# Attention beside a gated linear unit on one core: in the last unit, the values' products as two sets of 64 rows in two PSUM banks

## The chip, the core and the metric

The kernel runs on one core of one Trainium2 chip. Its time is the device time in microseconds (us) of one execution; several executions give a median. The profile is that of one execution, with its records laid out by engine: PE is TensorE (PEld its weight loads), DVE is VectorE, ACT is ScalarE, POOL is GpSimd and SP is SyncE, which issues the DMAs.

## What is computed

The reference mixes two branches over the same `x` (2048 rows of 512) by a gate for each row. Branch A is attention with 32 query heads of width 16 that share one key head and one value head, followed by an output projection. Branch B is a linear unit with a sigmoid gate and an inner width of 1792. All is float32.

```python
q = (x @ wq).reshape(B, S, 32, 16).transpose(0, 2, 1, 3)
k, v = x @ wk, x @ wv
p = softmax(einsum("bhqd,bkd->bhqk", q, k) * 16 ** -0.5)
a = einsum("bhqk,bkd->bhqd", p, v).transpose(0, 2, 1, 3).reshape(B, S, 512) @ wo
b = (sigmoid(x @ w_gate) * (x @ w_up)) @ w_down
g = sigmoid((x * gate_w).sum(-1, keepdims=True))
return g * a + (1 - g) * b
```

## The kernel before

**Units and chunks.** The queries are worked in 32 units (NU): four blocks of 512 rows, and eight groups of four heads in each. A unit walks over 16 chunks (NC) of 128 keys. Of each chunk there are four score matmuls, one for each head (`scores`, L1096 to L1103, the matmul at L1101), with the keys in the rows and one 64-row half of TensorE's array each; two in opposite halves make a pair. ScalarE takes the exponential of each from its PSUM bank into an SBUF tile `p` of 128 keys by 512 queries (L1103). Row maxima are found ahead of it by another pass of matmuls whose banks VectorE reduces (`maximum`, L1087 to L1094); the last unit's maxima are done before the stretch that this study looks at.

**The values' products.** `pv` (L974 to L977) takes the four `p` tiles of one chunk. Each is the moving operand of one f32 matmul over all 128 rows; the stationary operand is the chunk of `v_aug`, 128 keys by 32 columns (16 values and ones that sum the exponentials). Head j writes partitions 32j to 32j + 31 of one bank, so four column tiles share the array. Such a matmul leaves two records in the profile: 32 units by 16 chunks by 4 heads are 2048 matmuls, and L977 has 4096 records. A unit's chunks are worked in runs, one to six chunks at a time, between scores and the matmuls of branch B and of the output projection (`fill`, L1060 to L1071, in opposite halves too). In the units before the last, each run's sums leave the bank by a ScalarE copy (L984) and are added up on GpSimd (L991). The last unit, number 31, keeps one bank open from its first chunk to its last.

**What orders the work.** The order on every engine is written out by hand: the string `ORDER` (L645 to L690) has a letter or hex digit for each step, `V` for the values of one chunk, hex digits for pairs of half-row matmuls. `plan` (L693) plays it on a `State`, which keeps planned times, hands out the eight PSUM banks (`take`, L173 to L178: the one that comes free first) and places the work of the other engines (`settle`, L395). Each engine then runs its instructions in that order and waits on semaphores for what it needs; at the end of the program the order is pinned (L1153 to L1161). A score's matmul waits until the exponential of the score that had its bank before is done. In the stretch at hand the banks hold scores, the open sums of the values, and the open sums of the output projection of the last block of rows (`wa`), one for each half.

**The last unit and the end.** The last unit's 16 chunks are worked in ten runs: chunk 0 directly behind the last chunks of unit 30; 1; 2; 3; 4 and 5; 6; 7 and 8; 9 and 10; 11 and 12; 13 to 15. Until the run of 7 and 8 begins, the projection's `wa` matmuls are worked between the scores, and ScalarE takes a scaled copy of their sums now and then (L1052). Then only scores and values are left. Behind the last chunk come twelve half-row matmuls of the last projection (`we`, L1071), each three of which VectorE adds to the output (L1034). The end of the kernel (L1122 to L1150) then serves the last unit: ScalarE copies the sums' bank in two halves of 256 columns (L1128), four transposes bring queries into the rows (L1130), VectorE takes reciprocals (L1135) and divides (L1137), two more transposes (L1139), copies (L1141), four f32 matmuls with the last rows of `wo` in opposite halves (L1144), and VectorE's last sums (L1148) with their stores.

Of the kernel before, what the change touches and what calls it, by code (L numbers as in the profile page):

```python
# [12 lines left out]
ALU = mybir.AluOpType  # L13
# [5 lines left out]
P = 128  # L19
# [5 lines left out]
NC = S // P  # L25
NG = H // 4
NU = NB * NG
# [8 lines left out]
HALF = (TOP, BOT)  # L36
# [75 lines left out]
class State:  # L112
# [60 lines left out]
    def take(self):  # L173

        i = self.free.index(min(self.free))
        assert self.free[i] <= self.now
        self.free[i] = NEVER
        return i  # L178
# [325 lines left out]
    def issue_v(self):  # L504
        u, c = divmod(self.vp, NC)
        if self.sum is None:
            self.sum = self.take()
        self.run_of.append(["values", u, c, not self.run_of, False, self.sum])
        self.acts.append(self.run_of[-1])
        self.now += VALUES  # L510
        self.done += VALUES
        self.held -= 4
        self.exps.pop(0)
        self.vp += 1
        if c == NC - 1:
            self.release()
# [176 lines left out]
def plan():  # L693
    s = State()
    for code in ORDER:
        s.step(code)
    return s.acts
# [3 lines left out]
def tile_kernel(ctx, tc, x_in, wq, wkv, wo, wg, wu, wd, consts_in, out):  # L701
    nc = tc.nc
# [13 lines left out]
    banks = [pp.tile([P, 512], F32, tag=f"bank{i}", name=f"bank{i}") for i in range(8)]  # L716
# [136 lines left out]
    v_aug = cp.tile([P, NC, 32], F32, name="v_aug")  # L853
# [117 lines left out]

    PT, VD, OT = {}, {}, {}

    def pv(u, c, start, stop, ps):  # L974

        for j in range(4):
            nc.tensor.matmul(ps[32 * j:32 * j + 32, :], v_aug[:, c, :], PT.pop((u, c, j)), start=start, stop=stop)  # L977

    SUMS, PARTS_OF = {}, {}
# [116 lines left out]
    def scores(h, n, i):  # L1096
# [8 lines left out]
    on_bank = lambda act: lambda *args: act(*args[:-1], banks[args[-1]])  # L1105
# [4 lines left out]
        "load": load_item, "w_hi": w_hi, "w": w_split, "x_hi": x_hi, "x": x_lo, "turn_x": turn_x,  # L1110
        "f": fill, "gate": gate, "gated": gated, "h": h_split, "part": part_of, "add": add_part, "out": send_out,
        "m": maximum, "max_finish": max_finish, "max_turn": on_bank(max_turn), "send_max": send_max, "s": scores,
        "values": on_bank(pv), "finish": on_bank(finish), "store": store, "sums": sums, "invert": invert, "send_inverse": send_inverse,
        "spread": spread, "divide": divide,
    }
    for what, *args in plan():
        acts[what](*args)
        if what == "values":
            end = args[-1]


    n0 = (NB - 1) * NT  # L1122
    spare = lambda name: ap.tile([P, TB], F32, tag="p", name=name, bufs=PB)
    end, rest = banks[end], [bank for i, bank in enumerate(banks) if i != end]
    ps = rest[3:]
    ou = [spare(f"ou_last{i}")[:, :2 * P] for i in range(2)]
    for i in range(2):
        nc.scalar.copy(ou[i], end[:, i * 2 * P:(i + 1) * 2 * P])  # L1128
    for t in range(NT):
        nc.tensor.transpose(rest[t // 2][:, part(t % 2)], ou[t // 2][:, part(t % 2)], ident)  # L1130
    o = []
# [68 lines left out]
```

## Time and profile before

| | |
|---|---|
| Times of three runs | 1600.48, 1600.30, 1599.23 us; median 1600.3 us |
| The profiled execution's own time | 1598.83 us |
| Its span, first to last instruction | 1597.1 us |
| Granted TensorE clock | 1.0 of full speed |
| Matmuls of the values, L977 | 4096 records, 491.3 us busy, mean 598 ns |
| Score matmuls, L1101 | 2048, mean 400 ns |
| Exponentials, L1103 | 2048, mean 652 ns |
| DMA | 102.31 MB, 64 GB/s over the span |

A timeline row has the start in us from the span's start, the length in us, engine, line, operation, the tiles (output <- inputs), shapes, and how many instructions follow each other under that row (x); in brackets the engine's idle time before it and what ended it. Lengths of records overlap: a matmul's record reaches to its last output, and the next one starts earlier, so the distance between starts is the time that the engine needs for one. The same is true of ScalarE and VectorE, whose records begin while the instruction ahead is still at work. A row of busy times has, for each engine, the us in which it was busy in the stretch and the number of instructions in it.

### The profile page before, as it was taken

To read this page: it belongs to the slowest core of one execution; us is meant where nothing else is said; L and a number is where in the kernel's file an instruction comes from. 1 tells how busy PE (TensorE), PEld (TensorE's weight loads), DVE (VectorE), ACT (ScalarE), POOL (GpSimd) and SP (SyncE) were. 2 spreads that over 40 slices of the span, in tenths; PEclk is the share of its full clock that TensorE was granted. 3 is DMA by queue.
4 is the path that set the end of the run, shared out by engine and by line. 5 is a ranking of instruction groups with operands and counts; after the bars stand their busy time and mean duration, and the time that the engine had idled before them with its cause. 6 is when DMAs were issued, how large, how long until landed. Compare 5 with 4: busy or idle time off the path is not lost.

```text
span 1597.1 us, 33902 instructions
## 1 busy us (share of the span) xinstructions
PE 1587.9 (99%) x12918; PEld 998.6 (63%) x12918; DVE 1392.0 (87%) x2372; ACT 1258.4 (79%) x2474; POOL 848.0 (53%) x708
## 2 busy tenths in 40 slices
PE   9999999999999999999999999999999999999998
PEld 7776665665656566566666566666656665656654
DVE  7999998998988989988998898889989998988832
ACT  4268778888878878879878877878987887878896
POOL 4254364558363664375745446454936366536463
PEclk9999999999999999999999999999999999999999
DMA  7621121115111212013411121111502021201111
GB/s 239 216 80 42 42 57 36 45 59 137 29 68 32 75 56 60 18 39 83 111 37 58 39 75 54 55 38 59 137 28 68 32 75 46 71 16 42 34 36 44
DMA packets 54678, 102.31 MB, mean 64 GB/s; under 512 B 18232, under 2 KB 19768, under 8 KB 53492
## 3 DMA queue, kind: packets, MB, share of 16 engines
q1 hardware_dynamic: 54516, 100.16, 21.0%
q8 instruction: 101, 1.65, 0.4%
q14 instruction: 61, 0.50, 0.1%
HBM read 74.05 MB, written 13.09 MB: 55 GB/s over the span
## 4 chain that ended last, share of the span: by engine, by line
PE 98%; ACT 0%; DVE 0%; DMA 0%; POOL 0%; issue 0%; DVEq 0%
PE bank L1071 31%; PE bank L977 29%; PE bank L1092 18%; PE bank L1101 16%; PE bank L838 4%; ACT p L1103 0%; PE bank L963 0%; PE bank L908 0%; DVE ba L1148 0%; DVE ba L1034 0%; DMA wkv_raw<-wkv 0%; POOL wkv_s L732 0%; DVE wkv_stack L869 0%; PE bank L1144 0%; DVEq L1196 0%
## 5 line engine op out<-in xcount | busy, mean ns | idle before, releaser
L1094 DVE TENSOR_REDUCE mx<-bank 128x1 f32<-128x512 f32 x2048 | 1257.4, 681 | 133.8 <-PE bank L1092 80.5
L1103 ACT ACTIVATE p<-bank 128x512 f32<-128x512 f32 x2048 | 1050.1, 652 | 2.6 <-PE bank L1101 0.4
L1101 PE MATMUL bank<-qs,ks 64*128 64x512 f32 x2048 | 698.0, 400 | 0.0
L1092 PE MATMUL bank<-ks,qs 62*128 62x512 f32 x2048 | 686.6, 406 | 0.0
L977 PE MATMUL bank<-p,v_aug 128*32 128x512 f32 x4096 | 491.3, 598 | 0.7 <-ACT p L1103 0.7
L1092 PEld LDWEIGHTS bank<-ks,qs 62*128 62x128 f32 x2048 | 338.4, 184 | 151.3 <-issue 51.1
L1101 PEld LDWEIGHTS bank<-qs,ks 64*128 64x128 f32 x2048 | 345.7, 185 | 105.5 <-ACT p L1103 29.9
L991 POOL TENSOR_TENSOR ou<-ou,ou 128x512 f32<-128x512 f32 x201 | 259.0, 1289 | 204.9 <-ACT ou L984 199.2
L984 ACT COPY ou<-bank 128x512 f32<-128x512 f32 x232 | 140.9, 608 | 266.6 <-PE bank L977 122.2
L1071 PE MATMUL bank<-wd,hl 64*128 64x512 f32 x1344 | 273.5, 393 | 0.0
L977 PEld LDWEIGHTS bank<-p,v_aug 128*32 128x32 f32 x4096 | 107.7, 109 | 232.2 <-issue 188.1
L1071 PEld LDWEIGHTS bank<-wd,hl 64*128 64x128 f32 x1344 | 195.0, 185 | 20.4 <-ACT p L1103 1.7
L1071 PE MATMUL bank<-xs,wg 64*128 64x512 f32 x672 | 203.2, 393 | 0.0
L1071 PE MATMUL bank<-xs,wu 64*128 64x512 f32 x672 | 199.7, 393 | 0.0
L1071 PE MATMUL bank<-x,wu 64*128 64x512 f32 x672 | 194.5, 391 | 0.0
L1071 PE MATMUL bank<-x,wg 64*128 64x512 f32 x672 | 190.4, 391 | 0.0
L1071 PEld LDWEIGHTS bank<-xs,wg 64*128 64x128 f32 x672 | 119.7, 185 | 8.1
L1071 PEld LDWEIGHTS bank<-xs,wu 64*128 64x128 f32 x672 | 118.6, 185 | 7.3
L1071 PEld LDWEIGHTS bank<-x,wu 64*128 64x128 f32 x672 | 115.5, 185 | 10.7 <-issue 1.7
L1071 PEld LDWEIGHTS bank<-x,wg 64*128 64x128 f32 x672 | 113.3, 185 | 9.4 <-POOL wu L814 0.8
L1055 POOL TENSOR_TENSOR ba<-ba,pa_d 128x512 f32<-128x512 f32 x48 | 61.8, 1288 | 95.9 <-DVE ba L1034 62.6
L813 POOL CAST wu<-ru 128x1024 fp32r<-128x1024 f32 x27 | 28.1, 1039 | 117.6 <-PE bank L1071 94.3
(83 smaller groups left out, 1064.1 us busy)
## 6 DMA issues: line engine op xcount, KB each, us to landing
rg<-wg SPq DMA_DIRECT2D x28, 512.0 KB
ru<-wu SPq DMA_DIRECT2D x28, 512.0 KB
rd<-wd SPq DMA_DIRECT2D x28, 512.0 KB
qs<-qd SPq DMA_DIRECT2D x192, 64.0 KB
qd<-q SPq DMA_DIRECT2D x32, 256.0 KB
xs<-x SPq DMA_DIRECT2D x16, 512.0 KB
xf<-x_in SPq DMA_DIRECT2D x16, 256.0 KB
ra<-wo SPq DMA_DIRECT2D x8, 512.0 KB
```

Source lines behind the costliest of these rows:

```text
L813: nc.gpsimd.tensor_copy(WS[item][:, 0, :], raw)
L838: nc.tensor.matmul(ps, w[:, p, part(kc)], X[b, kc][:, q, :], start=i == 0, stop=i == 3 * KC - 1)
L977: nc.tensor.matmul(ps[32 * j:32 * j + 32, :], v_aug[:, c, :], PT.pop((u, c, j)), start=start, stop=stop)
L984: nc.scalar.copy(to, ps)
L991: nc.gpsimd.tensor_tensor(SUMS[u], SUMS[u], PARTS_OF[u].pop(0), op=ALU.add)
L1055: nc.gpsimd.tensor_tensor(BA[b, t], BA[b, t], PA.pop((b, t)), op=ALU.add)
L1071: nc.tensor.matmul(banks[i], l, r, start=at == 0, stop=at == j.n - 1)
L1092: nc.tensor.matmul(banks[i], qs_t[u % 3][r, pr, part(qt)], ks[r, kb * 512:(kb + 1) * 512], start=True, stop=True)
L1094: nc.vector.tensor_reduce(MX[u][:, pr, h, qt, kb:kb + 1], banks[i], axis=AX.X, op=ALU.max)
L1101: nc.tensor.matmul(banks[i], ks[r, part(c)], qs_t[u % 3][r, pr, :], start=True, stop=True)
L1103: nc.scalar.activation(p, banks[i], AF.Exp, scale=0.25)
```

## The change

In unit 31 alone, each chunk's product is worked as two sets of four matmuls: the first over key rows 0 to 63 into one bank, the second over rows 64 to 127 into a second bank. Both banks stay open over all 16 chunks, so the planner takes one bank more at the unit's first chunk; where no bank is free at the planned time, its clock moves on to the time at which one is. At the end ScalarE copies the first bank as before, and VectorE adds the second bank to each half of the copy before the transposes. Banks are numbered otherwise from then on, and the order of the instructions on each engine is otherwise that of before: TensorE has 64 matmuls more, VectorE the two adds.

```diff
     def take(self):
         i = self.free.index(min(self.free))
+        if self.vp >= (NU - 1) * NC:
+            self.now = max(self.now, self.free[i])
         assert self.free[i] <= self.now
...
         if self.sum is None:
             self.sum = self.take()
+            if u == NU - 1:
+                self.other = self.take()
...
+        if u == NU - 1:
+            self.run_of[-1][0] = "halves"
+            self.run_of[-1].append(self.other)
...
-    def pv(u, c, start, stop, ps):
-
-        for j in range(4):
+    def pv(u, c, start, stop, ps, *other):
+
+        for h, bank in enumerate((ps, *other) if other else ()):
+            for j in range(4):
+                nc.tensor.matmul(bank[32 * j:32 * j + 32, :], v_aug[HALF[h], c, :], PT[u, c, j][HALF[h]],
+                                 start=start, stop=stop)
+        for j in range(0 if other else 4):
             nc.tensor.matmul(ps[32 * j:32 * j + 32, :], v_aug[:, c, :], PT.pop((u, c, j)), start=start, stop=stop)
...
-    end, rest = banks[end], [bank for i, bank in enumerate(banks) if i != end]
-    ps = rest[3:]
+    two, rest = [banks[i] for i in end], [bank for i, bank in enumerate(banks) if i not in end]
+    ps = [rest[3], two[0], rest[4], rest[5]]
...
     for i in range(2):
-        nc.scalar.copy(ou[i], end[:, i * 2 * P:(i + 1) * 2 * P])
+        nc.scalar.copy(ou[i], two[0][:, i * 2 * P:(i + 1) * 2 * P])
+        nc.vector.tensor_tensor(ou[i], ou[i], two[1][:, i * 2 * P:(i + 1) * 2 * P], op=ALU.add)
```

More of the change, by code (lines that the diff above doesn't have):

```diff
@@ L1112, in tile_kernel @@
         "m": maximum, "max_finish": max_finish, "max_turn": on_bank(max_turn), "send_max": send_max, "s": scores,
-        "values": on_bank(pv), "finish": on_bank(finish), "store": store, "sums": sums, "invert": invert, "send_inverse": send_inverse,
+        "values": on_bank(pv), "halves": lambda u, c, a, b, *two: pv(u, c, a, b, *(banks[i] for i in two)), "finish": on_bank(finish), "store": store, "sums": sums, "invert": invert, "send_inverse": send_inverse,
         "spread": spread, "divide": divide,
@@ L1117, in tile_kernel @@
         acts[what](*args)
-        if what == "values":
-            end = args[-1]
+        if what == "halves":
+            end = args[-2:]
     n0 = (NB - 1) * NT
     spare = lambda name: ap.tile([P, TB], F32, tag="p", name=name, bufs=PB)
-    end, rest = banks[end], [bank for i, bank in enumerate(banks) if i != end]
-    ps = rest[3:]
+    two, rest = [banks[i] for i in end], [bank for i, bank in enumerate(banks) if i not in end]
+    ps = [rest[3], two[0], rest[4], rest[5]]
     ou = [spare(f"ou_last{i}")[:, :2 * P] for i in range(2)]
     for i in range(2):
-        nc.scalar.copy(ou[i], end[:, i * 2 * P:(i + 1) * 2 * P])
+        nc.scalar.copy(ou[i], two[0][:, i * 2 * P:(i + 1) * 2 * P])
+        nc.vector.tensor_tensor(ou[i], ou[i], two[1][:, i * 2 * P:(i + 1) * 2 * P], op=ALU.add)
     for t in range(NT):
```

## The prediction

> **What bounds the kernel now.** The page first, for its span, the busy times and the chain that ended last.
>
> ```profile
> span 1597.1 us, 33902 instructions
> PE 1587.9 (99%) x12918; PEld 998.6 (63%) x12918; DVE 1392.0 (87%) x2372; ACT 1258.4 (79%) x2474; POOL 848.0 (53%) x708
> PE 98%; ACT 0%; DVE 0%; DMA 0%; POOL 0%; issue 0%; DVEq 0%
> ```
>
> Over the whole span TensorE is the bound. But the change touches only the last unit, whose values' products begin at about 1552 us, so I read that stretch by itself: busy times of the window between its first free exponential and its last one, then the chain inside it.
>
> ```profile
> core 0: us, PE busy (x) PEld busy (x) DVE busy (x) ACT busy (x) POOL busy (x), PEclk, DMA share, GB/s
> 1553.43:1583.75 30.32, 29.67 (x239) 13.78 (x235) 3.17 (x5) 30.32 (x61) 15.65 (x15) 1.00 0.11 23
> ```
>
> ```profile
> 1575.80 7.95 ACT p L1103 x16
> ...
> 1583.80 1.06 PE bank L977 x8
> ```
>
> ScalarE is busy 30.32 of 30.32 us there (57 exponentials and four scaled copies): in this stretch it is the bound, and TensorE, though its row says 98%, runs just ahead of it. So an edit on TensorE matters here only if it leaves ScalarE without scores. Behind 1583.75 comes a serial end: the last values, the last output projection, sums, divide, store.
>
> **The rows for the terms.** TensorE's timeline, start and length in us; each matmul of the values leaves two records (two passes), so x8 is one key chunk and x16 two.
>
> ```profile
> 1550.18 2.78 PE L977 MATMUL bank<-p,v_aug 128*32 128x512 f32 x24
> 1552.89 0.49 PE L1101 MATMUL bank<-qs,ks 64*128 64x512 f32 x1
> ...
> 1568.39 0.40 PE L1071 MATMUL bank<-wa,o 64*128 64x512 f32 x2
> 1568.72 1.06 PE L977 MATMUL bank<-p,v_aug 128*32 128x512 f32 x8
> 1569.72 0.72 PE L1101 MATMUL bank<-qs,ks 64*128 64x512 f32 x3
> 1570.06 1.31 PE L1071 MATMUL bank<-wa,o 64*128 64x512 f32 x9
> ...
> 1572.59 0.41 PE L1101 MATMUL bank<-qs,ks 64*128 64x512 f32 x2
> 1572.93 1.92 PE L977 MATMUL bank<-p,v_aug 128*32 128x512 f32 x16
> 1574.78 0.97 PE L1101 MATMUL bank<-qs,ks 64*128 64x512 f32 x6
> ...
> 1583.80 1.06 PE L977 MATMUL bank<-p,v_aug 128*32 128x512 f32 x8 [0.70 <-ACT p L1103]
> 1584.79 3.03 PE L1071 MATMUL bank<-we,o 64*128 64x512 f32 x12
> 1587.75 0.66 PE L1130 MATMUL bank<-consts,ou_last 128*128 128x128 f32 x4
> ...
> 1589.94 1.99 PE L1144 MATMUL bank<-re,o_last 64*128 64x512 f32 x8
> ```
>
> Two chunks last 1574.78 - 1572.93 = 1.85 us, one 1569.72 - 1568.72 = 1.00: a chunk costs **0.86 us**, a run of them 0.14 beside. Pairs of half-row matmuls follow each other 0.23 apart (twelve single ones in 3.03 give 0.25), but the last pair before a run starts 0.33 ahead of it, and the first after it takes 0.34: each run pays about 0.1 + 0.14 + 0.1 = **0.35 us** for going to 32-column tiles and back. ScalarE's timeline:
>
> ```profile
> 1552.23 1.11 ACT L984 COPY ou<-bank 128x512 f32<-128x512 f32 x1
> 1553.42 7.46 ACT L1103 ACTIVATE p<-bank 128x512 f32<-128x512 f32 x15
> 1560.59 0.86 ACT L1052 ACTIVATE pa_a<-bank,gsig 128x512 f32<-128x512 f32 x1
> 1561.16 4.21 ACT L1103 ACTIVATE p<-bank 128x512 f32<-128x512 f32 x8
> 1565.00 0.95 ACT L1052 ACTIVATE pa_a<-bank,gsig 128x512 f32<-128x512 f32 x1
> ...
> 1573.53 0.90 ACT L1052 ACTIVATE pa_a<-bank,gsig 128x512 f32<-128x512 f32 x1
> ```
>
> An exponential takes 0.49 us of ScalarE (8 in 1565.00 - 1561.16 give 0.48, 16 in 7.95 give 0.50), a scaled copy 0.57 (1561.16 - 1560.59).
>
> **The change, part by part.** Each engine keeps its order of instructions: TensorE has 4 matmuls more in each of 16 chunks, VectorE two adds more, and the banks are numbered anew. No DMA, nothing on GpSimd or SyncE moves.
>
> *1. The products.* The 64x32 tile is in no row of before. Each half still streams 512 columns in two passes, so a set of four can't take less than the 0.86 us of today: no gain by itself. If the upper and the lower set run beside each other, a chunk stays at 0.86; if one follows the other, it is 1.72. Two rows speak for beside: the four f32 matmuls at L1144 lie in opposite halves by turns and need 1.99 us, where four in a row would need 4 x 0.86 = 3.44; and four column tiles share one chunk's 0.86 at L977. I take **0**, and keep +0.86 per chunk as the other end.
>
> *2. The switches.* Values and scores are now both of 64 rows, which might spare the 0.35 us per run; or the narrower columns cost it as before. No row shows a change of columns alone. Between 0 and 0.35 I take 0.35, what every run in the rows pays. The Trainium skill (TensorEngine Tiling, Key Properties) says that a change of the tiling mode, not of the tile, drains TensorE, and lists 64x32 and 64x128 as two modes: by that rule the switch stays, which agrees with the 0.35 of the rows and speaks against a gain here. New is one switch between the last chunk of unit 30, still 128 rows, and chunk 0 of unit 31, today one run (x24): about 0.1, with the longer first pass and the eight starts 0.15. ScalarE is out of scores just then (copy until 1553.34, next exponential at 1553.42), so it counts: **+0.15**.
>
> *3. One bank less for scores.* Of eight banks one holds the values' sums and two the output projection's sums in flight until 1572.6; five are left for scores, after the change four. Over a run of two chunks no score is written for 1574.78 - 1572.59 = 2.19 us; a score's exponential starts 0.53 after it (1552.89 to 1553.42), and a bank is TensorE's again about 0.16 after ScalarE has gone on (an exponential's row is 0.60 long at its shortest against 0.49 between them, and 0.05 from 1583.75 to 1583.80). ScalarE must have 2.19 + 0.53 + 0.16 = 2.88 us of work in the banks. Five exponentials and a scaled copy are 5 x 0.49 + 0.57 = 3.02: enough, as the full window shows. Four are 2.53: 0.35 idle. That happens at the runs 1563.41 and 1572.93 (scaled copies at 1565.00 and 1573.53): **+0.7**, between 0 and one exponential each, 1.0. Runs of one chunk need 0.86 less, 2.02 against 4 x 0.49 = 1.96: 0.06 each for four of them, **+0.2**. From 1574 on no projection is in flight, six banks are left, 2.94 against 2.88: nothing. A ScalarE that is full elsewhere can't win any of it back.
>
> *4. The two adds.* VectorE's rows of the end, and the groups by shape:
>
> ```profile
> 1585.86 2.82 DVE L1034 SCALAR_TENSOR_TENSOR ba<-bank,gsig,ba 128x512 f32<-128x512 f32 x4 [12.22 <-PE bank L1071]
> 1588.60 0.20 DVE L1135 RECIPROCAL rc_last<-bank 128x8 f32<-128x8 f32 x1
> ```
>
> ```profile
> L1148 DVE SCALAR_TENSOR_TENSOR ba<-bank,gsig,ba 128x256 f32<-128x256 f32 x2 | 0.9, 480 | 1.5 <-PE bank L1144 1.5
> ...
> L1137 DVE TENSOR_TENSOR on<-bank,rc_last 128x128 f32<-128x128 f32 x2 | 0.6, 290 | 0.1
> ```
>
> The plan's four sums of the last projection are issued ahead of the adds, so these stand in VectorE's queue behind the sum that waits for the twelfth projection matmul. Today the transposes (1587.75, 0.66 long) lie beside that last sum, and the reciprocal starts 0.67 after it has begun (four starts 0.69 apart put it at 1587.93). Afterwards: sum 0.67, first add 0.48 (the 128x256 row; the 128x128 one, 0.29, bounds it below, a 128x512 sum, 0.75, above), 0.05, two transposes 0.44, 0.07: the reciprocal starts 1.71 after it, **+1.05**. The second add (0.40 further) and its transposes lie beside the first half's division. With the adds at 0.29 it is +0.85, at 0.75 +1.3. The two ScalarE copies are done by 1585.6 and hidden. Nothing hides the adds: each step behind them waits for the one before.
>
> Sum: 0.15 + 0.7 + 0.2 + 1.05 = **+2.1 us**. The profiled execution took 1598.8 (span 1597.1 and 1.7 around it), after it 1600.9. The median of the runs shown is 1600.3, 1.5 higher than that execution; against it I forecast **1602.4 us**, 0.13% more. A measurement of this kernel can tell about 0.2%, 3.2 us, from no change.
>
> **The rivals.**
>
> *No switch is paid.* If only the rows count, a run of two needs 2.88 - 0.35 = 2.53 and four banks just do; terms 2 and 3 go to nothing, and the projection behind the last chunk starts 0.2 to 0.3 earlier. The adds stay: +0.8, **1601.1**. For it: all neighbours are of 64 rows. Against it: every run in the rows pays, and none shows which dimension it pays for.
>
> *The sets run one after the other* (the other side: slower). Place: each chunk; price: 0.86; it decides as soon as the tiles of the lower half can't stream while the four of the upper do. 16 x 0.86 = 13.7, less the 0.70 that TensorE waits at 1583.80, with adds, first switch and some starving +14.6: **1614.9**. Then the change doesn't do what it says. Against it the L1144 and L977 rows, but each shows one dimension split, never both.
>
> *The lower set runs one pass late.* If matmuls start strictly in order and both passes of one go ahead of the next, the lower four start 0.43 behind, and each run ends 0.43 later. The two runs of term 3 then lose 0.78 each, the next two 0.37 each, three single ones 0.49, the first 0.58, the last chunk 0.43: 4.8 with the adds' 1.05 **+5.8, 1606.1**. The Trainium skill (TensorE: Matmul & The Clock Gate, Part 3, The mechanism) says that matmuls start and end strictly in the order of the program. The 0.86 of a chunk today, though, has no room for one tile a pass behind another.
>
> *Faster.* The adds alone cost 0.85 to 1.3 and ScalarE has no idle time to give back; to win 3.2 us the exponentials themselves would have to shorten.
>
> **How the numbers follow.** Forecast 0.48; no switch 0.24; one pass late 0.12; one after the other 0.13; faster 0.03. Within 0.2%: 0.48 + 0.24 = 0.72; slower 0.25; faster 0.03. The range runs from 1600.0 (no switch, less the 1.1 by which the runs shown scatter) to 1606.5 (one pass late) and leaves out 0.16.
>
> **What would show it.** A run of two chunks still about 1.9 us with twice the records means term 1 is right; 2.3 the late pass, 3.6 one after the other. The first score pair behind a run still taking 0.34 means the switch stayed; 0.23 that it went. ScalarE idle about 0.35 near 1566 and 1576, and none behind it, shows term 3; a full row refutes it. Two adds between the last sum and the first reciprocal, with 1.7 instead of 0.67 between their starts, show term 4. I am wrong if the time lies in chunks that grew, or in VectorE rows far from 0.48.

## The result, and the profile after

| | before | after |
|---|---|---|
| Median of 18 runs each | 1600.72 us (1599.09 to 1602.18) | 1603.24 us (1601.75 to 1605.31) |
| Ratio of the runs, 95% interval | | 1.0017, 1.001 to 1.0025 |
| The profiled execution's own time, span | 1598.83, 1597.1 us | 1603.01, 1601.2 us |
| Mean granted TensorE clock of the profiled execution | 1.0 | 0.998 |

The changed kernel is **2.5 us slower** (interval 1.6 to 4.0); 1602.4 was forecast. In this kernel `pv`'s 64-row matmul is L985 (L988 over 128 rows), scores are L1112, their exponentials L1114, the projections L1082, scaled copies L1063, the last projection's sums L1045, the adds L1140, the transposes L1142, reciprocal and division L1147 and L1149, the last f32 matmuls L1156.

TensorE's timeline of the changed kernel, columns as before (start, length, engine, line, tiles, shapes, count, idle time before):

```profile
1572.82 0.62 PE L1082 MATMUL bank<-wa,o 64*128 64x512 f32 x4
...
1575.03 1.95 PE L985 MATMUL bank<-p,v_aug 64*32 64x512 f32 x32
1576.90 0.97 PE L1112 MATMUL bank<-qs,ks 64*128 64x512 f32 x6
1577.80 1.95 PE L985 MATMUL bank<-p,v_aug 64*32 64x512 f32 x32
1579.68 1.35 PE L1112 MATMUL bank<-qs,ks 64*128 64x512 f32 x6
1580.96 1.95 PE L985 MATMUL bank<-p,v_aug 64*32 64x512 f32 x32
...
1585.99 1.09 PE L985 MATMUL bank<-p,v_aug 64*32 64x512 f32 x16 [0.30 <-ACT p L1114]
1587.01 3.01 PE L1082 MATMUL bank<-we,o 64*128 64x512 f32 x12
1591.26 0.78 PE L1142 MATMUL bank<-consts,ou_last 128*128 128x128 f32 x4 [1.24 <-DVE ou_last L1140]
1592.32 0.92 PE L1151 MATMUL bank<-consts,on 128*128 128x128 f32 x2 [0.29 <-DVE on L1149]
1593.17 3.35 PE L1156 MATMUL bank<-re,o_last 64*128 64x512 f32 x8
```

A run of two chunks has 32 records instead of 16 and lasts 1.95 us instead of 1.92: the two sets do run beside each other. Two rows are new in kind: the transposes wait 1.24 us for the add, and the last f32 matmuls (x8), 1.99 before, last 3.35. ScalarE's timeline:

```profile
1552.84 1.11 ACT L995 COPY ou<-bank 128x512 f32<-128x512 f32 x1
1554.21 7.81 ACT L1114 ACTIVATE p<-bank 128x512 f32<-128x512 f32 x15 [0.26 <-PE bank L1082]
1561.93 0.69 ACT L1063 ACTIVATE pa_a<-bank,gsig 128x512 f32<-128x512 f32 x1
1562.52 4.04 ACT L1114 ACTIVATE p<-bank 128x512 f32<-128x512 f32 x8
1566.40 0.73 ACT L1063 ACTIVATE pa_a<-bank,gsig 128x512 f32<-128x512 f32 x1
1567.49 4.51 ACT L1114 ACTIVATE p<-bank 128x512 f32<-128x512 f32 x9 [0.37 <-PE bank L1112]
...
1575.23 0.86 ACT L1063 ACTIVATE pa_a<-bank,gsig 128x512 f32<-128x512 f32 x1
1575.80 1.27 ACT L1114 ACTIVATE p<-bank 128x512 f32<-128x512 f32 x2
1577.43 8.50 ACT L1114 ACTIVATE p<-bank 128x512 f32<-128x512 f32 x17 [0.36 <-PE bank L1112]
```

ScalarE, full before, now stands idle twice for 0.36 to 0.37 us, behind the runs of two chunks that were named, and needs 1561.93 - 1554.21 = 7.72 us for the first 15 exponentials (7.17 before, 1553.42 to 1560.59). VectorE's rows of the end:

```profile
1588.07 2.80 DVE L1045 SCALAR_TENSOR_TENSOR ba<-bank,gsig,ba 128x512 f32<-128x512 f32 x4 [12.37 <-PE bank L1082]
1590.79 0.74 DVE L1140 TENSOR_TENSOR ou_last<-ou_last,bank 128x256 f32<-128x256 f32 x2
1591.74 0.21 DVE L1147 RECIPROCAL rc_last<-bank 128x8 f32<-128x8 f32 x1 [0.20 <-PE bank L1142]
...
1595.28 2.85 DVE L1160 SCALAR_TENSOR_TENSOR ba<-bank,gsig,ba 128x256 f32<-128x256 f32 x5 [2.57 <-PE bank L1156]
```

The adds stand where they were expected, and the reciprocal starts 1591.74 - 1590.12 = 1.62 us behind the start of the last sum (1590.12 in the chain of waits of this kernel), 0.67 before. The sums behind the last matmuls wait 2.57 us. Why the last matmuls are slow is told by busy times in two stretches of 3.41 us (each engine's busy time and count, then the granted clock, PEclk):

```profile
1589.12:1592.53 3.41, 1.88 (x9) 0.94 (x8) 3.14 (x9) 0.00 (x0) 0.00 (x0) 1.00 0.00 0
1592.53:1595.94 3.41, 3.30 (x10) 1.37 (x9) 0.84 (x3) 0.53 (x2) 0.00 (x0) 0.50 0.02 5
```

The granted clock was 0.5 from 1592.53 to 1595.94, which holds the last matmuls but for their end. In the profile of before it fell only at 1595.66, when they had long been done; two stretches of that profile ahead of the fall:

```profile
1588.84:1592.25 3.41, 2.57 (x10) 0.96 (x10) 1.84 (x6) 0.53 (x2) 0.00 (x0) 1.00 0.00 0
1592.25:1595.66 3.41, 0.00 (x0) 0.00 (x0) 1.70 (x3) 0.00 (x0) 0.00 (x0) 1.00 0.85 308
```

Nothing of this was forecast.

**Where the time came from, in the trace.** Executions differ ahead of the last unit too: the last run of unit 30 (before: the row at 1550.18) starts between 1550.18 and 1552.85 in the profiles below, a difference that is there within the first 100 us and then stays (one of the kernels below is 2.4 late at 100 us and 2.5 here). In the two profiles that are over 2 us late, TensorE is slow in the first 12 us: nine f32 matmuls that last 2.33 us in before (at 7.33) last 3.46 there in one (the adds early, at 7.80) and 3.74 in the other (TensorE kept busy). So I measure each profile from that start, call it R, to the end of VectorE's last sum:

| us | before | after |
|---|---|---|
| R to the end of the last exponential | 33.56 | 35.13 (+1.57) |
| from there to the start of the last of the four sums | 4.19 | 4.19 |
| from there to the first reciprocal | 0.67 | 1.62 (+0.95) |
| from there to the last f32 matmuls | 1.34 | 1.43 (+0.09) |
| from there to the first final sum | 1.16 | 2.11 (+0.95) |
| from there to the end of VectorE | 2.85 | 2.85 |
| sum | 43.77 | 47.33 (+3.56) |

### The profile page after: what moved, and what is told of

Read it like the earlier page. It is cut to its first block, busy times and chain, and to the rows that moved or that the text cites. A ratio compares the mean times of both kernels' runs of the same rounds, so it can differ in the third digit from the quotient of the medians.

```text
span 1601.2 us, 34160 instructions
## 1 busy us (share of the span) xinstructions
PE 1592.3 (99%) x13046; PEld 1001.2 (63%) x13046; DVE 1392.3 (87%) x2374; ACT 1259.0 (79%) x2474; POOL 848.3 (53%) x708
## 4 chain that ended last, share of the span: by engine, by line
PE 98%; ACT 1%; DVE 1%; DMA 0%; SPq 0%; issue 0%; POOL 0%; DVEq 0%
PE bank L1082 31%; PE bank L988 29%; PE bank L1103 18%; PE bank L1112 15%; PE bank L845 3%; PE bank L985 1%; ACT p L1114 1%; PE bank L970 0%; SPq L958 0%; DMA qs<-qd 0%; DVE ba L1160 0%; ACT x L763 0%; PE bank L1156 0%; DVE ba L1045 0%; DMA wkv_raw<-wkv 0%
## 5 line engine op out<-in xcount | busy, mean ns | idle before, releaser
L1114 ACT ACTIVATE p<-bank 128x512 f32<-128x512 f32 x2048 | 1050.2, 651 | 3.7 <-PE bank L1112 0.9
L1112 PE MATMUL bank<-qs,ks 64*128 64x512 f32 x2048 | 700.2, 401 | 0.0
L988 PE MATMUL bank<-p,v_aug 128*32 128x512 f32 x3968 | 475.6, 598 | 0.0
L1112 PEld LDWEIGHTS bank<-qs,ks 64*128 64x128 f32 x2048 | 346.6, 185 | 106.7 <-ACT p L1114 34.5
L1082 PE MATMUL bank<-wd,hl 64*128 64x512 f32 x1344 | 273.6, 393 | 0.0
L988 PEld LDWEIGHTS bank<-p,v_aug 128*32 128x32 f32 x3968 | 104.8, 109 | 223.7 <-issue 181.5
L1082 PEld LDWEIGHTS bank<-wd,hl 64*128 64x128 f32 x1344 | 195.3, 185 | 20.3 <-ACT p L1114 1.7
L1082 PE MATMUL bank<-xs,wg 64*128 64x512 f32 x672 | 203.3, 393 | 0.0
L1082 PE MATMUL bank<-xs,wu 64*128 64x512 f32 x672 | 199.3, 393 | 0.0
L1082 PE MATMUL bank<-x,wu 64*128 64x512 f32 x672 | 194.6, 392 | 0.0
L1082 PE MATMUL bank<-x,wg 64*128 64x512 f32 x672 | 190.7, 391 | 0.0
L1082 PEld LDWEIGHTS bank<-xs,wg 64*128 64x128 f32 x672 | 120.0, 185 | 7.2
L1082 PEld LDWEIGHTS bank<-xs,wu 64*128 64x128 f32 x672 | 118.5, 185 | 7.7
L1082 PEld LDWEIGHTS bank<-x,wu 64*128 64x128 f32 x672 | 115.6, 186 | 11.6 <-issue 1.7
L1082 PEld LDWEIGHTS bank<-x,wg 64*128 64x128 f32 x672 | 113.5, 186 | 8.9 <-POOL wu L821 0.8
```

What stands on the lines that cost most here:

```text
L1082: nc.tensor.matmul(banks[i], l, r, start=at == 0, stop=at == j.n - 1)
L1112: nc.tensor.matmul(banks[i], ks[r, part(c)], qs_t[u % 3][r, pr, :], start=True, stop=True)
L1114: nc.scalar.activation(p, banks[i], AF.Exp, scale=0.25)
```

## The experiments

My theory after the result: three costs that add up, 1.6 for the bank and the first switch, 0.95 for the adds, and about 1 for the clock, whose cause is that TensorE waits for the adds. The rivals: the halves themselves cost time somewhere; or the clock has nothing to do with the waiting. The first four kernels ran on one chip beside before (median 1599.99 us of 33 runs, 1598.91 to 1601.78).

**Two VectorE operations alone**, on the kernel before. The maximum of a copy and the bank that it was copied from leaves the values as they are.

```diff
         nc.scalar.copy(ou[i], end[:, i * 2 * P:(i + 1) * 2 * P])
+        nc.vector.tensor_tensor(ou[i], ou[i], end[:, i * 2 * P:(i + 1) * 2 * P], op=ALU.max)
```

> The kernel before, with one edit: behind each ScalarE copy of the last sums VectorE takes the maximum of the copy and the bank it came from (128x256 each), which leaves the values as they are. Products and banks are those of before, so this is term 4 by itself. Theory (the adds stand behind the last projection's sums in VectorE's queue and nothing hides them): the first reciprocal starts 1.6 to 1.7 us after the last of the four sums starts (0.67 before), about +1.0 us; from the last of the scores' exponentials back nothing moves, 31.8 us from the start of chunk 0 of the last unit to the end of the last exponential as before. If the granted clock falls to half while TensorE waits, as it did in the changed kernel's profile at 1592.5 us, another +0.9: up to +2.0. Rival (the adds are hidden beside the sums and the time is in the products): within 0.3 us of before.

Measured: 1602.71 us (1601.71 to 1604.78), ratio 1.0016 (1.0007 to 1.0025). In the trace the last exponential ends as in before (33.57 from R); the reciprocal starts 1.86 behind the last sum (the second copy shares the bank with the operation ahead and waits for it). The whole stretch is 46.69, 2.92 over before. Of TensorE's timeline of this kernel and its busy times, columns as above:

```profile
1589.40 0.58 PE L1131 MATMUL bank<-consts,ou_last 128*128 128x128 f32 x2 [1.24 <-DVE ou_last L1129]
...
1591.99 3.79 PE L1145 MATMUL bank<-re,o_last 64*128 64x512 f32 x8
```

```profile
1586.16:1589.57 3.41, 2.17 (x10) 1.46 (x9) 3.15 (x5) 0.19 (x1) 0.00 (x0) 1.00 0.00 0
1589.57:1592.98 3.41, 2.73 (x8) 1.20 (x9) 1.33 (x5) 0.71 (x3) 0.00 (x0) 0.50 0.02 5
```

The operations cost far more than the 1.05 of the prediction, in a kernel without halves and with all its banks: the same fall to 0.5 is here, for 6.83 us, and the last matmuls take 3.79. The halves are not needed for it.

**The bank alone.** The changed kernel, whose planner takes a second bank for the last unit, but with the products of before, over 128 rows, and without the adds.

```diff
-        "values": on_bank(pv), "halves": lambda u, c, a, b, *two: pv(u, c, a, b, *(banks[i] for i in two)), "finish": on_bank(finish), "store": store, "sums": sums, "invert": invert, "send_inverse": send_inverse,
+        "values": on_bank(pv), "halves": lambda u, c, a, b, i, other: pv(u, c, a, b, banks[i]), "finish": on_bank(finish), "store": store, "sums": sums, "invert": invert, "send_inverse": send_inverse,
...
-        nc.vector.tensor_tensor(ou[i], ou[i], two[1][:, i * 2 * P:(i + 1) * 2 * P], op=ALU.add)
```

> The changed kernel's plan with its second bank held open from the last unit's first chunk, but the products of before: four matmuls over all 128 rows into the first bank, nothing in the second, no adds. This is term 3 by itself, without term 2. Theory (one bank less starves ScalarE): idle time of 0.3 to 0.4 us at the runs of chunks 4 and 5 and of 7 and 8, from the start of chunk 0 to the end of the last exponential 32.6 to 33.1 us against 31.8 before and 33.3 in the changed kernel; time +0.8 to +1.3 us. Rival (the bank is not missed, the lengthening of that stretch is the 64x32 products and their switches): 31.8 us and no change of the time.

Measured: 1600.90 us (1600.37 to 1602.37), ratio 1.0006 (0.9998 to 1.0015). The last exponential ends 34.85 after R, 1.29 later than in before, and everything behind it lasts as in before (whole stretch 44.98, +1.21). ScalarE's timeline of this kernel shows the starving without a single half product:

```profile
1553.59 7.78 ACT L1114 ACTIVATE p<-bank 128x512 f32<-128x512 f32 x15
...
1566.81 4.52 ACT L1114 ACTIVATE p<-bank 128x512 f32<-128x512 f32 x9 [0.33 <-PE bank L1112]
...
1576.71 8.47 ACT L1114 ACTIVATE p<-bank 128x512 f32<-128x512 f32 x17 [0.33 <-PE bank L1112]
```

So 1.29 of the changed kernel's 1.57 ahead of the last exponential are the bank; the rest, 0.28, holds the first switch (0.17: the exponentials behind it start 1554.21 - 1550.80 = 3.41 after R, 3.24 before); the other 0.11 may come from the runs, each 0.02 to 0.03 longer, which is not shown. The clock stays at 1.0 until the matmuls are done.

**The adds early.** The changed kernel, but with the copies and the adds issued directly behind chunk 15, ahead of the last projection's sums, so that they lie beside its matmuls.

```diff
         if what == "halves":
             end = args[-2:]
+            if args[1] == NC - 1:
+                ou = [spare(f"ou_last{i}")[:, :2 * P] for i in range(2)]
+                for i in range(2):
+                    nc.scalar.copy(ou[i], banks[end[0]][:, i * 2 * P:(i + 1) * 2 * P])
+                    nc.vector.tensor_tensor(ou[i], ou[i], banks[end[1]][:, i * 2 * P:(i + 1) * 2 * P], op=ALU.add)
```

> The changed kernel with the two copies and the two adds issued directly behind the last chunk's products, ahead of the last projection's four sums in VectorE's queue. Theory (the adds cost only by their place in the queue): they run at about 0.35 us behind the copies, beside the twelve projection matmuls; the first reciprocal starts again 0.6 to 0.8 us after the last sum, and the time falls by 0.9 us against the changed kernel, by up to 1.9 if TensorE's clock then stays at full; against before +0.7 to +1.6. Rival (the adds are hidden already, or the chain waits for something else): the time of the changed kernel, +2.5.

Measured: 1602.71 us (1601.52 to 1604.57), ratio 1.0017 (1.0008 to 1.0026). The adds are hidden: the reciprocal starts 0.65 behind the last sum, as in before. But the whole stretch is still 46.42, +2.65, because the clock fell in this profile too (1594.07 to 1597.48), although TensorE had no adds to wait for:

```profile
1590.66:1594.07 3.41, 2.50 (x14) 1.47 (x12) 2.96 (x8) 0.27 (x1) 0.00 (x0) 1.00 0.00 0
1594.07:1597.48 3.41, 3.41 (x9) 1.10 (x8) 1.40 (x3) 0.27 (x1) 0.00 (x0) 0.50 0.01 2
```

That speaks against half of my theory: the wait for the adds is not the only way to a fall. Nor is the fall in every run of this kernel. Each run's mean granted clock is known; the profile's, 0.998, is one of the two lowest of its eleven runs, and five of them have 1.0. Those five take 1601.61 to 1602.71 us, the other six 1601.52 to 1604.57; how much of the difference is the clock and how much the start of the kernel can't be told from the times.

**TensorE kept busy while it waits.** The changed kernel with five matmuls of 128x128 between the last projection and the transposes, whose sums nobody reads.

```diff
+    for _ in range(5):
+        nc.tensor.matmul(two[0][:, :P], v_aug[:, :4, :], v_aug[:, 4:8, :], start=True, stop=True)
     for t in range(NT):
         nc.tensor.transpose(rest[t // 2][:, part(t % 2)], ou[t // 2][:, part(t % 2)], ident)
```

> The changed kernel with five f32 matmuls of 128x128 by 128 columns ahead of the last unit's transposes, on constants at hand, into the first sums' bank, which ScalarE has copied; their result is not used. They fill about 1.1 us of the time in which TensorE waits for the adds. Theory of the clock (the granted clock fell to 0.5 at the end because TensorE waited too long): the clock stays at 1.0 to the last matmul, the four last f32 matmuls need 2.0 us instead of 3.35, and the profile's end comes 0.9 us earlier than the changed kernel's, +1.5 against before. Rival (the clock falls for another reason, such as the end of the scores): 3.35 us again and the changed kernel's time, or 0.1 more for the matmuls.

Measured: 1603.14 us (1601.40 to 1604.45), ratio 1.0016 (1.0007 to 1.0025). In TensorE's timeline the extra matmuls fill the wait, and the last ones are short again; the clock is 1.0 until 1601.48:

```profile
1591.98 1.38 PE L1142 MATMUL bank<-v_aug 128*128 128x128 f32 x10
1593.29 0.77 PE L1144 MATMUL bank<-consts,ou_last 128*128 128x128 f32 x4
1594.36 0.77 PE L1153 MATMUL bank<-consts,on 128*128 128x128 f32 x2 [0.29 <-DVE on L1151]
1595.06 1.99 PE L1158 MATMUL bank<-re,o_last 64*128 64x512 f32 x8
```

The whole stretch is 46.22, +2.45: the 1.57 and 0.95 of the changed kernel without its third cost, which so comes to 3.56 - 2.45 = 1.1. The 0.09 between the reciprocal and the last matmuls belongs to it: here that step takes 1.29 (1.34 before), and its two transposes last 0.77 where they last 0.92 in the changed kernel. The median doesn't show that gain. It lies 3.1 above before's, where the expectation had put the profile's end at +1.5, and its interval (1.1 to 4.0 us) holds 2.45 as well as 3.56. To see a cost of 1 us in medians, I took it out of kernels where less else is changed. The second four kernels ran beside before at 1599.99 us again (27 runs, 1599.07 to 1602.25).

**The two operations, TensorE kept busy.** The first experiment with four such matmuls ahead of the transposes.

```diff
+    for _ in range(4):
+        nc.tensor.matmul(ps[1][:, :P], v_aug[:, :4, :], v_aug[:, 4:8, :], start=True, stop=True)
```

> The kernel before (values over 128 rows, one bank) with two VectorE operations ahead of the transposes (maxima of the copies and the same bank: values unchanged), as in the run with the two operations alone, and four extra matmuls of 128x128 in an unused bank while TensorE waits for them; nothing is left out. Theory: the two operations cost 0.95 us, and the 1.6 us that the run without the extra matmuls lost behind the reciprocal was the granted clock at 0.5 alone. Then the clock stays 1.0 until the last matmuls are done, these take 1.99 us again instead of 3.79, the stretch from unit 30's last run to VectorE's end is 43.77 + 1.0 = 44.8 us (that run: 46.4), and the median is 1.0 over before's. Rival: the loss of that run's median (+2.7) does not come from the clock: the median stays at +2.7 although the trace shows a full clock.

Measured: **1601.13 us** (1600.39 to 1602.85), ratio 1.0008 (0.9999 to 1.0017), where the same kernel without the extra matmuls had 1602.71. The clock stays at 1.0 until 1597.08. Of TensorE's timeline:

```profile
1588.41 1.16 PE L1131 MATMUL bank<-v_aug 128*128 128x128 f32 x8
...
1591.90 1.99 PE L1147 MATMUL bank<-re,o_last 64*128 64x512 f32 x8
```

The reciprocal is as late as without them (1.85 behind the last sum), but the last matmuls start 1.46 behind it instead of 1.86, and the first final sum 1.16 behind them instead of 2.11. The stretch is 45.07, +1.30 (44.8 was expected; the wait of the second copy makes up most of the rest), against the 46.69 of the run without (the expectation put that at 46.4). Work for TensorE that nothing uses takes 1.6 us off in the trace, and the medians differ by as much (their intervals over before, 1.1 to 4.0 and -0.2 to 2.7 us, still overlap). The rival falls: that part of the loss came from the clock.

**The adds early, TensorE kept busy.** The third experiment with two such matmuls behind the transposes.

```diff
         nc.tensor.transpose(rest[t // 2][:, part(t % 2)], ou[t // 2][:, part(t % 2)], ident)
+    for _ in range(2):
+        nc.tensor.matmul(two[0][:, :P], v_aug[:, :4, :], v_aug[:, 4:8, :], start=True, stop=True)
```

> The changed kernel with its copies and adds issued ahead of the last projection's sums (so that they lie beside its matmuls) and two extra matmuls of 128x128 in an unused bank while TensorE waits for the first division; nothing is left out. Theory: the adds are hidden and the clock stays full, so that only the bank and the first switch are left: exponentials end 1.55 us later, everything behind them lasts as before, the stretch is 43.77 + 1.55 = 45.3 us, the median 1.2 to 1.6 over before's. Rival: a cost of the change lies elsewhere (in code or data ahead of the last unit): the median is again 2.7 over before's.

Measured: 1601.63 us (1600.97 to 1603.22), ratio 1.0009 (1.0 to 1.0018). The exponentials end 35.12 after R (+1.56), the reciprocal starts 0.66 behind the last sum, the last matmuls take 1.99 us, and the whole stretch is 45.30, +1.53. With the adds hidden and the clock kept, what is left of the change is the bank and the first switch, and the median (+1.6) agrees.

**The changed kernel a second time**, for another profile of it.

> The changed kernel once more, for a second profile of the same program. Theory (the clock falls by windows of 3.41 us whose place varies between executions): all stretches up to the reciprocal repeat within 0.1 us (exponentials end 1.57 later than before's, reciprocal 1.62 behind the last sum's start), while the stretch behind it is 1.43 + 2.11 or 1.34 + 1.16 by whether a fall lands in it; where it does, it lasts 3.41 or twice that. Rival (the fall is set by the program): again 0.5 from the last f32 matmuls' start on, for 3.41 us.

Measured: 1602.77 us, span 1601.0. The exponentials end 35.12 after R, the reciprocal starts 1.61 behind the last sum: both repeat. The clock fell again, earlier against the work and for longer:

```profile
1588.17:1591.58 3.41, 2.15 (x11) 1.19 (x9) 3.18 (x8) 0.00 (x0) 0.00 (x0) 1.00 0.00 0
1591.58:1594.99 3.41, 3.13 (x8) 1.55 (x10) 0.80 (x4) 0.53 (x2) 0.00 (x0) 0.50 0.00 0
1594.99:1598.40 3.41, 1.50 (x4) 0.00 (x0) 2.77 (x5) 0.00 (x0) 0.00 (x0) 0.50 0.51 183
```

It then stayed at 0.5 to the end of the span, where the expectation allowed 3.41 us or twice that. The stretch from R is 47.58, +3.81: here the last pair of matmuls ran at 0.5 to its end, 0.26 more than in the first profile. So in two profiles of two the fall comes in time to cost 1.1 and 1.4 us, though its place and length move. The other runs have no trace; what their mean clocks say stands under the table at the end of this section.

**ScalarE relieved**, on the kernel before. The prediction read the last 30 us as bound by ScalarE alone. Here VectorE, with little to do there, adds the last block's projection sums straight from their banks, without ScalarE's scaled copies.

```diff
-        if how == "sum":
+        if how == "sum" or how == "apart" and j.kind == "a" and b == NB - 1:
             add(banks[i], b, t, scale)
             return
...
     def add_part(_, b, t):
+        if (b, t) not in PA:
+            return
```

> The kernel before, in which ScalarE makes no scaled copies of the last projection's sums in the last block: VectorE, with 3.17 us of work in the 30.3, adds them straight from the bank; nothing is left out. Theory of the prediction (ScalarE alone bounds the 30 us of the last unit): four copies of 0.57 go, the last exponential ends 2.3 us earlier, the median is 2 below before's. Rival (TensorE runs so close ahead that it is the bound as soon as ScalarE is faster; PE is busy 29.67 of 30.32): ScalarE gets idle time in place of the copies, the last exponential ends within 0.5 us of before's, the median within 0.5.

Measured: 1600.25 us (1599.22 to 1603.34), ratio 1.0002 (0.9993 to 1.0011). The last exponential ends 34.03 after R, 0.47 later than in before, the stretch is 44.15, +0.38. Busy times from the first free exponential to the last, and two rows of ScalarE's timeline:

```profile
1553.73:1584.51 30.78, 30.05 (x239) 13.97 (x235) 6.16 (x9) 28.59 (x57) 10.57 (x11) 1.00 0.11 23
```

```profile
1566.04 6.00 ACT L1105 ACTIVATE p<-bank 128x512 f32<-128x512 f32 x12 [0.56 <-PE bank L1103]
...
1576.07 8.44 ACT L1105 ACTIVATE p<-bank 128x512 f32<-128x512 f32 x17 [1.28 <-PE bank L1103]
```

And two of TensorE's:

```profile
1569.93 0.73 PE L1103 MATMUL bank<-qs,ks 64*128 64x512 f32 x3
1570.74 1.42 PE L1073 MATMUL bank<-wa,o 64*128 64x512 f32 x9
```

ScalarE has four instructions less and is idle for 30.78 - 28.59 = 2.19 us, about what they took (4 x 0.57 = 2.28). TensorE is busy 30.05 of 30.78. The edit also makes TensorE wait once for VectorE: the projection's matmuls behind the scores at 1569.93 start 0.81 later, when VectorE has read the second of two banks (1569.08, 1.60 us for both), where in before they start 0.34 later (1569.72 to 1570.06). That is the 0.47; without it the last exponential would end as in before, by estimate, and not 2.3 earlier. So in this stretch both engines are at their bound at once: the row of before that shows ScalarE at 30.32 of 30.32 was right, and the conclusion that TensorE had room was not.

All runs together, the stretch measured from R in one profile each:

| kernel | median, us | over before | stretch over before | lowest PEclk up to the last matmuls | runs with a mean clock of 0.998 or less |
|---|---|---|---|---|---|
| changed | 1603.24 | +2.5 | +3.56, +3.81 | 0.5 | 12 of 18 |
| two operations alone | 1602.71 | +2.7 | +2.92 | 0.5 | 9 of 11 |
| bank alone | 1600.90 | +0.9 | +1.21 | 1.0 | 1 of 11 |
| changed, adds early | 1602.71 | +2.7 | +2.65 | 0.5 | 2 of 11 |
| changed, kept busy | 1603.14 | +3.1 | +2.45 | 1.0 | 0 of 11 |
| two operations, kept busy | 1601.13 | +1.1 | +1.30 | 1.0 | 0 of 11 |
| changed, adds early, kept busy | 1601.63 | +1.6 | +1.53 | 1.0 | 0 of 11 |
| ScalarE relieved | 1600.25 | +0.3 | +0.38 | 1.0 | 0 of 11 |

The last column is from all runs, not from one profile each; beside them 4 of before's 60 runs have 0.998 or less. A mean counts the end of the kernel too, behind the last matmuls, where a low clock costs nothing, so a single run's figure doesn't say whether a fall came in time. But the kernels differ: where TensorE waits for the operations on VectorE 21 of 29 runs are that low, with the bank alone or the adds early 3 of 22, and with TensorE kept busy none of 33. So the falls in the profiles are no accident of a few executions.

## Why the prediction was right, and where it was not

**The total.** +2.1 forecast, +2.5 measured, and the case named likeliest is the one that came. Part of that is luck: the forecast's own terms measure 2.5 us in the trace (1.57 + 0.95, and 2.45 with TensorE kept busy), and the clock, which was in no term, adds 1.1 and 1.4 in the two profiles. The median, whose interval is 1.6 to 4.0, can't tell 2.5 from 3.6.

**1. The products, 0: right.** 1.95 us with 32 records against 1.92 with 16. A late pass would have shown 2.3, one set after the other 3.6; neither came. The Trainium skill (TensorE: Matmul & The Clock Gate, Part 3, The mechanism) was the ground for the late pass, with its strict order of starts; in the changed kernel's trace all eight tiles of a chunk start within 0.05 us, and the second passes 0.43 to 0.45 behind them. The trace shows nothing against the order of the starts; what fails is the rival's own condition that both passes of one matmul go ahead of the next.

**2. The switches, as before and one more: right.** The run and the first scores behind it cost what they did: from the start of a run of two to the next score 1576.90 - 1575.03 = 1.87 (1.85 before), and the first score pair behind a run still takes 0.34 (1566.96 to 1567.30). "No switch is paid" falls. The new switch at chunk 0 measured 0.17 against 0.15.

**3. A bank less for scores, 0.9: right in kind, too small.** Both runs of two chunks starve ScalarE as worked out, 0.37 and 0.36 us where 0.35 was given. Mis-sized were the runs of one chunk: the first 15 exponentials, with the chunks 1 to 3 among them, took 0.55 more, where the term had 0.2 for four such runs. The requirement was taken from before's rows, in which the last scores ahead of a run are in good time; with a bank short, that score itself can start late, and the run behind it with it: ahead of chunk 1 three scores last 0.86 us instead of 0.62, and the run starts 0.79 behind the first of them (1554.49 to 1555.28) instead of 0.55. That nothing would be lost from 1574 on was also a little off: the scores behind the next run took 1.35 us for six instead of 0.96 (1579.68), and the stretch from the fourth scaled copy to the last exponential grew by 0.49, of which 0.36 are the named idle. The bank by itself, in the experiment that changes nothing else, costs 1.29.

**4. The adds, 1.05: right.** 0.95 measured. The first add holds the transposes for 0.42 us (the chain of waits) instead of 0.48, and the second one, as forecast, costs nothing at the division: with the clock kept at 1.0 that step takes 1.29 us (1.34 before).

**What failed: "Nothing hides the adds: each step behind them waits for the one before" counted their time and not what TensorE does meanwhile.** The step took every duration behind the adds from the profile of before, at its clock of 1.0. In the changed kernel TensorE stands idle for 1.24 us ahead of the transposes, which followed at once before, the granted clock falls to 0.5 for a stretch of 3.41 us, and the last four f32 matmuls, which everything waits for, run at half speed: the term that the sum lacks is 1.1 us. Two experiments show it from both sides: the operations without the halves bring the fall (+2.92 in the trace, a mean clock of 0.996 to 0.999 in its eleven runs), and matmuls that do nothing but fill the wait take it away (+1.30, and 0.999 to 1.0).

**The bound.** That ScalarE alone is the bound and TensorE "runs just ahead of it" was wrong as a reading: with ScalarE 2.3 us lighter nothing was won. It did little harm to the sum, since the halves cost TensorE only 0.02 to 0.03 us for each run.

**What stays open.** What exactly makes the clock fall. The stretches of 3.41 us ahead of a fall had TensorE busy for 1.88, 2.15, 2.17 and 2.50 us; four ahead of which it stayed full had 2.57 (before), 2.54 (the bank alone), 2.28 (kept busy) and 2.08 (early and kept busy). Busy time alone doesn't part them. One count does, but it was found only afterwards, and no run tests it: leave out the transposes, and take half of the time of the twelve projection matmuls, which have 64 rows each and come one behind the other (the last f32 matmuls lie in both halves at once). Then the four ahead of a fall hold 0.45, 0.69, 1.00 and 0.70 us (in the same order), the four others 1.99, 1.38, 1.99 and 1.99; but the edge is narrow, as a stretch with ScalarE relieved (1586.44 to 1589.85) holds 1.07 and the clock stayed full. Nor do I know why the clock fell in the profile of the kernel with the adds early, whose TensorE waits no longer than before's; that the boundary of the stretch lay elsewhere against the work would explain it, and would fit its other runs, of which five have a mean clock of 1.0; it was not tried.

## What to carry to other kernels

A wait added ahead of TensorE's last matmuls can cost more than its own length: here 0.95 us of adds brought a fall of the clock that cost 1.1 more. Look at the granted clock behind such a wait, and try matmuls that fill it. An engine that is busy throughout a stretch is not shown to be its only bound; take load off it in an experiment before planning by it. Where executions scatter by as much as the effect, measure the touched stretch in the trace from a mark ahead of it, and use the medians as the check.

## What the runs showed of the hardware

**The granted clock fell within the kernel's last microseconds while TensorE was still at work.** It fell to 0.5 for 3.41 us in two profiles, 6.83 us in a third, and to the end of the matmuls in a fourth, behind stretches in which TensorE was busy 55 to 73% of the time. At 0.5, a pass of the 512-column f32 matmuls took 0.85 instead of 0.43 us. The Trainium skill (TensorE: Matmul & The Clock Gate, Part 1, What's actually happening) gives a free-running window of 3413 ns, after an idle one of which the clock is halved. The length agrees with the 3.41 of the traces; "idle" doesn't, as none of the windows ahead of a fall was.

**Eight column tiles of 64 rows worked at once.** Eight f32 matmuls in tiles of 64x32 took the 0.86 us of a chunk that four of 128x32 took, and from the start of a run of two chunks to the next score 1.87 us passed instead of 1.85.
